# Running two stages' products, then two stages' outputs, in a fused attention and mixture kernel on one Trainium2 core

## The chip, the core and the metric

One NeuronCore of a Trainium2 chip runs the whole program. Its engines work side by side, each through its own list of instructions in the order in which the program wrote them: PE (matrix products, with weight loads shown as PEld), DVE (element-wise work, reads the products' accumulators), ACT (activations, copies and rounding, reads the accumulators too), POOL (element-wise work on SBUF) and SP (which issues most DMAs). An engine whose next instruction waits for a semaphore holds up everything behind it in its own list. The metric is device time of one execution in microseconds (us).

## The reference: what is computed

Three layers follow each other: block-causal attention, a mixture of eight experts with weights from a Sinkhorn-like normalisation, and a squared-ReLU feed-forward layer.

```python
# attention: batch 4, heads 8, 576 positions, head size 64, blocks of 64
attn = softmax over allowed blocks of (q k^T / 8);  x = (attn v) as [2304, 512]
# mixture ("layer one"): 8 experts, each 512 -> 1024 -> 512
P = exp(x @ w_gate - max); 8 rounds of normalising rows and columns of P
out = sum over e of P[:, e:e+1] * (relu(x @ w1[e]) @ w2[e])
# feed-forward ("layer two"): 512 -> 2048 -> 512, weights given as float64
g = relu(x @ w_in) ** 2
return g @ w_out
```

## The kernel before

**Tiling.** The 2304 tokens are cut into three groups of 768 (`NG = 3`), each of six tiles of 128 tokens (`GT = 6`). A *stage* takes one group and one slice of 256 hidden columns: 32 stages per group in layer one (8 experts times 4 slices), 8 in layer two. The list `stages` has 120 entries S: 0 to 95 are layer one (three groups of 32), 96 to 119 layer two (three groups of 8).

**A stage** has two halves on PE. First come seven *products* (function `product`), one for each of the seven terms of a Strassen-like scheme (`PRODUCTS`, called m1, m2, m6, m7, m4, m5, m3 in the order in which they run). Each is six matmuls of 384 columns, L346 to L348 twice, since both operands are split into a rounded part and a remainder (`ah`, `al` for the weights, `x` for the input). Then come six *output tiles* (function `output`), each of six matmuls of 512 columns, L401 to L403 twice, that multiply the hidden tile `h` by the second weight `b`.

**What the products feed.** Each product lies in one PSUM bank until its reader is through. m1 is copied to SBUF by ACT (L357); the others are read by DVE additions (L352), which form sums u2, u3, u4 and four tiles `c`. Each `c` becomes hidden values (`hidden`): in layer one ACT applies ReLU with rounding (L314) and DVE forms the remainder (L315). In layer two three of the four `c` of a stage take two more steps on ACT, ReLU and square (L320, L321), before the rounding (L324); the first one is squared by DVE (L323). DVE's remainder there is L325. Remainders are put in the queue `wait` and written into DVE's list a little later: `product` empties the queue after m1, m2, m6, m7, m4 and m5, and `output` takes one entry at tile `PUTOFF = 3`.

**Where products lie.** `Turns` hands out banks to products in rotation over five places: four single banks (`sc00` to `sc11`) and, as fifth, the pool `ps`, whose four banks are shared with the output tiles, themselves in rotation. A product therefore needs, four times out of five, that the product five before it has been read; an output tile needs that the holder of the bank four before it in the shared pool has been read.

**What else runs.** Weights come as float32 and are split on chip. `conv_a` splits one of the seven first-weight combinations for a stage: ACT rounds (L197) and POOL forms the remainder (L198). `sums` forms four combinations on POOL (L181). `conv_b` splits half of the second weight (ACT L205, POOL L206); `load` brings the raw weights, one buffer for `w2` and two for `w1`. `form` builds the next group's seven input combinations (POOL L265, ACT L271, L272 on POOL or DVE). `conv64` turns layer two's float64 weights into float32 during layer one (DVE L222 to L240, POOL L225).

**What sets the order.** The program keeps a list `pieces`; each piece is a product or an output tile with the helpers attached to it. `fill` walks through it, and after each piece takes steps of the queues `gate`, `slow` (`conv64`, every `SLOW`-th piece), `forming` (`fetch` and `form`, every `pace`-th piece) and `side` (`stage_work`: `conv_b`, `sums`, loading). From stage 5 on the order is `RUNS`: the seven products of stage S, then the six output tiles of stage S-1. In `products(S)`, the weights of stage S+1 are split one product behind the product that used the same buffer (`conv_a(S + 1, ...)`).

Of the kernel before, what the change touches and what calls it, by code (L numbers as in the profile page):

```python
# [25 lines left out]
NG = 3  # L26
GT = NTILE // NG
GN = 64 * GT
NMOE = 32
NST = 40  # L30
# [13 lines left out]
PRODUCTS = [(1, 0, 0), (2, 1, 1), (6, 4, 4), (7, 5, 5), (4, 2, 6), (5, 3, 3), (3, 6, 2)]  # L44
# [54 lines left out]
PUTOFF = 3  # L99
# [3 lines left out]
DLO = (0, 3, 6, 9, 12)  # L103

GATE = 1

SLOW = 4

# [16 lines left out]
def fused_kernel(ctx: ExitStack, tc: tile.TileContext, q, k, v, wg, w1, w2, u1, u2, ident, out):  # L125
# [24 lines left out]
    stages = [  # L150
        (g, s, layer * NG + g)
        for layer, (s0, s1) in enumerate(((0, NMOE), (NMOE, NST))) for g in range(NG) for s in range(s0, s1)
    ]
# [17 lines left out]
    def sums(S):  # L171
        if S >= len(stages):
            return
        r = raw["w1", S].rearrange("p (f d) -> p f d", f=2)
        a11, a12, a21, a22 = r[:, 0, 0:256], r[:, 0, 256:512], r[:, 1, 0:256], r[:, 1, 256:512]
        t = wsum[S] = rawp.tile([128, 4, 256], F32, tag="sum", name="sum")
        for z, (o, x, y, op) in enumerate((
            (0, a21, a22, ALU.add), (1, t[:, 0], a11, ALU.subtract), (2, a11, a21, ALU.subtract),
            (3, a12, t[:, 1], ALU.subtract),
        )):  # L180
            nc.gpsimd.tensor_tensor(out=t[:, o], in0=x, in1=y, op=op)  # L181
            if z == 1:
                yield
        yield
# [146 lines left out]
    def in_runs(S):  # L331
        return EARLY < S < NG * NST

    def product(S, j):
        g, s, q = stages[S]
        m, ia, ib = PRODUCTS[j]
        if j == 0:
            ht[S] = [[hpool.tile([128, 2 * GN], F32R, tag=f"h{f}{z}", name=f"h{f}{z}", bufs=2) for z in range(2)]
                     for f in range(2)]
            while q not in formed:  # L340
                assert step_of(forming)
        p = extra["ps"].tile([128, 512], F32, tag="g", name="m")[:, :GN]
        ah, al = wa[S, ia]
        bh, bl = (t[:, ib] for t in xop[q % 2])
        for k2 in range(2):
            nc.tensor.matmul(p, ah[:, k2], bh[:, k2], start=(k2 == 0), stop=False)  # L346
            nc.tensor.matmul(p, ah[:, k2], bl[:, k2], start=False, stop=False)  # L347
            nc.tensor.matmul(p, al[:, k2], bh[:, k2], start=False, stop=(k2 == 1))  # L348

        def add(tag, other, pool=tmp):  # L350
            t = pool.tile([128, GN], F32, tag=tag, name=tag)
            nc.vector.tensor_tensor(out=t, in0=p, in1=cur[other], op=ALU.add)  # L352
            return t

        if m == 1:
            cur["m1"] = tmp.tile([128, GN], F32, tag="mu", name="m1")
            nc.scalar.activation(out=cur["m1"], in_=p, func=ACTF.Copy)  # L357
            flush_wait()
        elif m == 2:
            x = add("c", "m1", cpool)  # L360
            flush_wait()
            hidden(S, 0, 0, x)
        elif m == 6:
            cur["u2"] = add("u2", "m1")
            flush_wait()
        elif m == 7:
            cur["u3"] = add("u3", "u2")
            flush_wait()
        elif m == 4:
            x = add("c", "u3", cpool)  # L370
            flush_wait()
            hidden(S, 1, 0, x)
        elif m == 5:
            cur["u4"] = add("mu", "u2")
            x = add("c", "u3", cpool)
            flush_wait()
            hidden(S, 1, 1, x)
        else:
            x = add("c", "u4", cpool)
            if not in_runs(S):  # L380
                flush_wait()
            hidden(S, 0, 1, x)
# [31 lines left out]
    def output(S, t):  # L414
        g, s, q = stages[S]
        if not in_runs(S + 1):
            flush_wait()
        elif wait and (t == PUTOFF or S == NG * NST - 2 and t == 1):
            wait.popleft()()
        while S not in ready_b:  # L420
            assert step_of(side)
        first = q == 0 and s < 8
        if q == 0 and s == 8:
            drain(gate)
        a = acc[1 if first and s >= 4 else q % 2][:, t]
        if S == len(stages) - 1 and t == GT - 1:
            last_tile(S, t, a, (g * GT + t) * 128)
            return
        p = ps.tile([128, 512], F32, tag="g", name="y")
        terms(p, S, t, slice(0, 512))  # L430

        e = s // 4
        tile_no = g * GT + t
        pe = prob[:, tile_no, e % NEXP:e % NEXP + 1]
        if s == NMOE:
            nc.vector.tensor_copy(out=a, in_=p)
        elif first and s % 4 == 0:
            nc.scalar.activation(out=a, in_=p, func=ACTF.Copy)
        elif s == 0:
            nc.scalar.activation(out=a, in_=p, func=ACTF.Copy, scale=pe)  # L440
        elif s > NMOE or first:
            nc.vector.tensor_tensor(out=a, in0=p, in1=a, op=ALU.add)
        else:
            if q == 0 and s == 8:
                nc.scalar.activation(out=a, in_=a, func=ACTF.Copy, scale=prob[:, tile_no, 0:1])
            nc.vector.scalar_tensor_tensor(out=a, in0=p, scalar=pe, in1=a, op0=ALU.mult, op1=ALU.add)  # L446
            if q == 0 and s == 8 + t // 2:
                nc.vector.scalar_tensor_tensor(
                    out=a, in0=acc[1][:, t], scalar=prob[:, tile_no, 1:2], in1=a, op0=ALU.mult, op1=ALU.add
                )  # L450
        if s == NMOE - 1:
            late.append((q, t))
        if len(late) > (2 if s == NMOE - 1 else 0):
            x2(*late.popleft())
        if s == NST - 1:
            r0 = tile_no * 128
            nc.sync.dma_start(out=out[r0:r0 + 128, :], in_=a)
# [4 lines left out]
    def piece(fn, us=0.0, need=None):  # L462
        pieces.append((need, us, fn))

    def products(S):
        res = []
        for j in range(7):
            def fn(j=j):
                product(S, j)
                if j == 0:  # L470
                    load("w1", S + 2)
                else:
                    conv_a(S + 1, PRODUCTS[j - 1][1])
                if j == 6:
                    conv_a(S + 1, PRODUCTS[6][1])
            res.append((0, 1.03, fn))
        return res

    def outputs(S):
        return [(0, 1.37, lambda t=t: output(S, t)) for t in range(GT)]  # L480

    def task(gen):
        piece(lambda: side.append(gen))
# [6 lines left out]
    def step_of(queue):  # L490
        while queue:
            if next(queue[0], "end") != "end":
                return True
            queue.popleft()
        return False
# [8 lines left out]
    def stage_work(S):  # L504

        conv_b(S, 0)
        if S + 1 < len(stages):
            yield from sums(S + 1)
            summed.add(S + 1)
        conv_b(S, 1)  # L510
        load("w2", S + 1)
        ready_b.add(S)
        yield

    pace = [1]

    def begin(S):
        side.append(stage_work(S))
        g, s, q = stages[S]
        layer = s >= NMOE  # L520
        at, every = FORM[layer]
        if s - (NMOE if layer else 0) == at and q + 1 < 2 * NG:
            forming.append(fetch(q + 1))
            pace[0] = every

    for S in range(len(stages) + 1):
        a = products(S) if S < len(stages) else []
        b = outputs(S - 1) if S else []
        if a:
            piece(lambda S=S: begin(S))  # L530
        for z in WEAVE if S <= EARLY else RUNS if in_runs(S) else BLOCKS:
            src = a if z == "m" else b
            if src:
                pieces.append(src.pop(0))
        pieces += a + b
        if S == EARLY:
            split = len(pieces)
    pos = [0]
    beat = [0]

    def fill(us, end):
        while us > 0 and pos[0] < end:
            need, cost, fn = pieces[pos[0]]
            if need is not None and need not in formed:
                return us
            fn()
            pos[0] += 1
            us -= cost
            if cost:
                beat[0] += 1  # L550
                for _ in range(GATE):
                    step_of(gate)
                if beat[0] % SLOW == 0 and not gate:
                    step_of(slow)
                if beat[0] % pace[0] == 0:
                    step_of(forming)
                step_of(side)
        return us

# [473 lines left out]
```

## Time and profile before

| | before |
|---|---|
| median of 3 runs | 2058.68 us (2058.38 to 2059.91) |
| the profiled execution's own time | 2058.25 us |
| its span, first to last instruction | 2056.5 us |
| TensorE's granted clock over the span | 1.000 (2.4 GHz) |
| PE busy | 2040.9 us, 99% of the span |
| DVE, POOL, ACT busy | 1620.9 us (79%), 1586.1 us (77%), 988.5 us (48%) |
| share of PE in the chain that ended last | 95% |

The span covers attention with the first stages woven into it, up to about 310 us, and then a regular stretch of products and output tiles up to the end. Busy time of PE counts overlapping matmuls once; one matmul's duration (335 or 391 ns) is longer than the distance from its start to the next one's start, so distances between starts tell more than durations. "Idle before" is time in which the engine did nothing, with what ended it.

### The profile page before, as it was taken

Reading aid. Unit: us, or ns where it says so; the run is one execution under the profiler, and the core shown is the slowest. Engines: PE = TensorE matmul, PEld = TensorE weight load, DVE = VectorE, ACT = ScalarE, POOL = GpSimd, SP = SyncE. Lnnn points to the kernel's source line nnn. Section 1 sums busy time; section 2 is a strip of 40 time slices with the busy share of each in tenths; the row PEclk is TensorE's granted clock in tenths of the full one; section 3 lists DMA queues with packets and bytes.
Section 4 is the critical chain, followed back from the end, with each engine's and each line's share of the span. In section 5 each row is a group of like instructions: output and inputs, shape, how many; then the busy total and the mean of one; then the engine's idle time right before and its main releaser. Section 6 shows DMA issues by size and latency. Waiting matters only on the chain.

```text
span 2056.5 us, 34155 instructions
## 1 busy us (share of the span) xinstructions
PE 2040.9 (99%) x11614; PEld 1813.2 (88%) x11614; DVE 1620.9 (79%) x2864; ACT 988.5 (48%) x2439; POOL 1586.1 (77%) x1786
## 2 busy tenths in 40 slices
PE   8999999999999999999999999999999999999999
PEld 5677898998999899899899999989989998998998
DVE  7887788888887678788888777888887677777776
ACT  8977444344343434334434343433443446656554
POOL 4564577798888778778888777878887778979874
PEclk9999999999999999999999999999999999999999
DMA  6543212322222322232223233233222123232311
GB/s 186 149 131 93 64 62 92 124 78 96 95 77 100 116 82 93 92 114 93 86 79 103 77 118 103 78 115 106 78 77 88 62 83 111 75 123 67 108 62 51
DMA packets 80862, 194.70 MB, mean 95 GB/s; under 512 B 26160, under 2 KB 27568, under 8 KB 80688
## 3 DMA queue, kind: packets, MB, share of 16 engines
q1 hardware_dynamic: 80544, 192.39, 28.3%
q8 instruction: 91, 1.49, 0.3%
q14 instruction: 83, 0.68, 0.1%
q10 hardware_dynamic: 144, 0.13, 0.0%
HBM read 169.95 MB, written 20.97 MB: 93 GB/s over the span
## 4 chain that ended last, share of the span: by engine, by line
PE 95%; DVE 3%; ACT 1%; issue 1%; POOL 0%; DMA 0%; SPq 0%; ACTq 0%; POOLq 0%; DVEq 0%
PE y L401 16%; PE y L402 16%; PE y L403 16%; PE m L346 14%; PE m L348 14%; PE m L347 14%; PE pv L750 1%; PE sc L626 1%; PE T L706 1%; DVE mx L645 1%; DVE pb L683 1%; ACT pb L667 0%; DVE nm L656 0%; PE x2t L392 0%; DVE sm L688 0%
## 5 line engine op out<-in xcount | busy, mean ns | idle before, releaser
L346 PE MATMUL m<-x,ah 128*128 128x384 f32 x1680 | 566.0, 337 | 0.4 <-DVE c L352 0.3
L401 PE MATMUL y<-b,h 128*128 128x512 f32 x1442 | 564.6, 392 | 0.9 <-DVE c L352 0.9
L403 PE MATMUL y<-b,h 128*128 128x512 f32 x1442 | 563.8, 391 | 0.0
L348 PE MATMUL m<-x,al 128*128 128x384 f32 x1680 | 563.5, 335 | 0.0
L402 PE MATMUL y<-b,h 128*128 128x512 f32 x1442 | 563.3, 391 | 0.0
L347 PE MATMUL m<-x,ah 128*128 128x384 f32 x1680 | 562.7, 335 | 0.0
L206 POOL TENSOR_TENSOR b<-raww,b 128x512 fp32r<-128x512 f32 x240 | 326.6, 1361 | 299.9 <-ACT b L205 296.6
L446 DVE SCALAR_TENSOR_TENSOR acc<-y,prob,acc 128x512 f32<-128x512 f32 x516 | 380.4, 746 | 132.1 <-PE y L403 127.4
L198 POOL TENSOR_TENSOR al<-sum,ah 128x256 fp32r<-128x256 f32 x480 | 392.4, 837 | 33.2 <-ACT ah L197 13.6
L357 ACT ACTIVATE m<-m 128x384 f32<-128x384 f32 x120 | 59.1, 492 | 634.1 <-PE m L348 634.1
L346 PEld LDWEIGHTS m<-x,ah 128*128 128x128 f32 x1680 | 315.7, 188 | 8.1 <-issue 0.5
L198 POOL TENSOR_TENSOR al<-raww,ah 128x256 fp32r<-128x256 f32 x360 | 307.0, 853 | 17.8 <-ACT ah L197 11.4
L403 PEld LDWEIGHTS y<-b,h 128*128 128x128 f32 x1442 | 270.7, 188 | 56.7
L347 PEld LDWEIGHTS m<-x,ah 128*128 128x128 f32 x1680 | 315.5, 188 | 4.7
L401 PEld LDWEIGHTS y<-b,h 128*128 128x128 f32 x1442 | 271.1, 188 | 54.4 <-DVE c L352 1.0
L402 PEld LDWEIGHTS y<-b,h 128*128 128x128 f32 x1442 | 270.9, 188 | 52.5
L348 PEld LDWEIGHTS m<-x,al 128*128 128x128 f32 x1680 | 315.4, 188 | 0.0
L315 DVE SCALAR_TENSOR_TENSOR h<-c,h 128x384 fp32r<-128x384 f32 x384 | 303.6, 791 | 3.7 <-ACT h L314 3.3
L314 ACT ACTIVATE h<-c 128x384 fp32r<-128x384 f32 x384 | 201.3, 524 | 179.0 <-DVE c L352 169.8
L197 ACT ACTIVATE ah<-sum 128x256 fp32r<-128x256 f32 x480 | 185.1, 409 | 128.0 <-POOL sum L181 119.0
L181 POOL TENSOR_TENSOR sum<-raww 128x256 f32<-128x256 f32 x240 | 198.7, 828 | 0.0
L352 DVE TENSOR_TENSOR c<-m,m 128x384 f32<-128x384 f32 x120 | 66.8, 557 | 106.2 <-ACT b L205 95.2
(117 smaller groups left out, 2416.3 us busy)
## 6 DMA issues: line engine op xcount, KB each, us to landing
raww<-w_t SPq DMA_DIRECT2D x192, 512.0 KB, 3.5
raww<-w1f SPq DMA_DIRECT2D x24, 512.0 KB, 3.5
raww<-w2f SPq DMA_DIRECT2D x24, 512.0 KB, 3.3
q<-q_d SPq DMA_DIRECT2D x15, 576.0 KB, 4.0
raw<-w_in_bits SPq DMA_DIRECT2D x16, 512.0 KB, 5.0
raw<-w_out_bits SPq DMA_DIRECT2D x16, 512.0 KB, 4.6
acc<-xd SPq DMA_DIRECT2D x30, 256.0 KB, 4.7
v<-v_p SPq DMA_DIRECT2D x16, 320.0 KB, 3.8
```

The costliest lines, as they stand in the source:

```text
L181: nc.gpsimd.tensor_tensor(out=t[:, o], in0=x, in1=y, op=op)
L198: nc.gpsimd.tensor_tensor(out=lo, in0=src, in1=hi.bitcast(F32), op=ALU.subtract)
L206: nc.gpsimd.tensor_tensor(out=lo[:, f], in0=src, in1=hi[:, f].bitcast(F32), op=ALU.subtract)
L314: nc.scalar.activation(out=hh, in_=x3, func=ACTF.Relu)
L315: wait.append(lambda: nc.vector.scalar_tensor_tensor(out=hl, in0=x3, scalar=0.0, in1=hh.bitcast(F32), op0=ALU.max, op1=ALU.subtract,))
L346: nc.tensor.matmul(p, ah[:, k2], bh[:, k2], start=(k2 == 0), stop=False)
L347: nc.tensor.matmul(p, ah[:, k2], bl[:, k2], start=False, stop=False)
L348: nc.tensor.matmul(p, al[:, k2], bh[:, k2], start=False, stop=(k2 == 1))
L401: nc.tensor.matmul(p, hh, bh[:, f, cols], start=(f == 0), stop=False)
L402: nc.tensor.matmul(p, hh, bl[:, f, cols], start=False, stop=False)
L403: nc.tensor.matmul(p, hl, bh[:, f, cols], start=False, stop=(f == 1))
L446: nc.vector.scalar_tensor_tensor(out=a, in0=p, scalar=pe, in1=a, op0=ALU.mult, op1=ALU.add)
```

## The change

From stage 12 on, stages go in pairs (S, S+1), S even: seven products of S, seven of S+1, then six output tiles of S and six of S+1. The numbers of instructions on PE, DVE and POOL stay as they are; their order changes. The `conv_a` of the odd stage stays in the products of the even one, that of the next even stage moves to the output tiles of the even one, and the products of the odd stage carry none. `sums` of the next pair's odd stage goes between the two runs of output tiles. Within pairs the steps of `slow` and `forming` are taken beside output tiles alone (`kind` "t"): `slow` at every second one, `forming` at every fifth in layer one and every second in layer two (`TFORM`). Two remainders are written at tiles 1 and 3 of the first run of output tiles of a pair (and of stage 10).

```diff
+TFORM = {False: 5, True: 2}
+
+TWO = 12
...
+    def is_pair(S):
+        return TWO <= S < NG * NST and S % 2 == 0
+
+    def twice(S):
+        return is_pair(S) or S in (TWO - 2, NG * NST - 2)
...
-        elif wait and (t == PUTOFF or S == NG * NST - 2 and t == 1):
+        elif wait and (t in (1, PUTOFF) if twice(S) else t == PUTOFF):
             wait.popleft()()
...
                 if j == 0:
                     load("w1", S + 2)
-                else:
+                elif not is_pair(S - 1):
                     conv_a(S + 1, PRODUCTS[j - 1][1])
-                if j == 6:
+                if j == 6 and not is_pair(S - 1):
                     conv_a(S + 1, PRODUCTS[6][1])
...
         conv_b(S, 0)
-        if S + 1 < len(stages):
-            yield from sums(S + 1)
-            summed.add(S + 1)
+        if S + 1 not in summed:
+            yield from add_up(S + 1)
+        else:
+            yield
+            yield
         conv_b(S, 1)
...
             pace[0] = every
+            tpace[0] = TFORM[layer]
...
+    def both(S):
+
+        for z in (S, S + 1):
+            piece(lambda z=z: begin(z))
+            pieces.append((None, 0.0, lambda: kind.__setitem__(0, "m")))
+            pieces.extend(products(z))
+        pieces.append((None, 0.0, lambda: kind.__setitem__(0, "t")))
+        ys = outputs(S)
+        for t, (need, us, fn) in enumerate(ys):
+            def more(t=t, fn=fn):
+                fn()
+                for j in (t, t + 1) if t == GT - 1 else (t,):
+                    conv_a(S + 2, PRODUCTS[j][1])
+            pieces.append((need, us, more))
+        task(add_up(S + 3))
+        pieces.extend(outputs(S + 1))
+        pieces.append((None, 0.0, lambda: kind.__setitem__(0, "")))
...
+        if is_pair(S):
+            if due is not None:
+                pieces += outputs(due)
+                due = None
+            both(S)
+            S += 2
+            continue
...
-                if beat[0] % SLOW == 0 and not gate:
-                    step_of(slow)
-                if beat[0] % pace[0] == 0:
-                    step_of(forming)
+                if kind[0] == "t":
+                    turns[0] += 1
+                    if turns[0] % 2 == 0 and not gate:
+                        step_of(slow)
+                    if turns[0] % tpace[0] == 0:
+                        step_of(forming)
+                elif kind[0] == "":
...
```

The lines of the changed program are shifted: PE's products are L356 to L358 there, its output tiles L411 to L413, ACT's copy of m1 L367, DVE's additions L362.

PE's list where the last stage's products begin, before: `y_24171` is an output tile of the stage two before it, `m_24183` the last stage's m1.

```order
L403 MATMUL y_24171<-b0_23847,h01_23832 128x512
L401 MATMUL y_24171<-b0_23847,h10_23833 128x512
L402 MATMUL y_24171<-b1_23848,h10_23833 128x512
L403 MATMUL y_24171<-b0_23847,h11_23834 128x512
L346 MATMUL m_24183<-x01_3738,ah_24038 128x384
L347 MATMUL m_24183<-x11_3739,ah_24038 128x384
```

The same place of the changed program: `m_24158` is the seventh product of the stage just before, `m_24182` the last stage's m1.

```order
L358 MATMUL m_24158<-x01_3738,al_24004 128x384
L356 MATMUL m_24158<-x01_3738,ah_24003 128x384
L357 MATMUL m_24158<-x11_3739,ah_24003 128x384
L358 MATMUL m_24158<-x01_3738,al_24004 128x384
L356 MATMUL m_24182<-x01_3738,ah_24088 128x384
L357 MATMUL m_24182<-x11_3739,ah_24088 128x384
```

The six output tiles that stood ahead of m1 are gone from there; the odd stage's products follow the even stage's with nothing between them.

DVE's list at the same place, before: from the `c` of the seventh product (`c_24117`) to the last stage's first two additions; `acc1` rows empty output tiles, `h` rows are remainders.

```order
L352 TENSOR_TENSOR c_24117<-m_24110,mu_24098 128x384
L442 TENSOR_TENSOR acc1_3737<-y_24130,acc1_3737 128x512
L442 TENSOR_TENSOR acc1_3737<-y_24138,acc1_3737 128x512
L442 TENSOR_TENSOR acc1_3737<-y_24146,acc1_3737 128x512
L325 TENSOR_TENSOR h11_24009<-c_24100,h10_24008 128x6x64
L442 TENSOR_TENSOR acc1_3737<-y_24155,acc1_3737 128x512
L442 TENSOR_TENSOR acc1_3737<-y_24163,acc1_3737 128x512
L442 TENSOR_TENSOR acc1_3737<-y_24171,acc1_3737 128x512
L325 TENSOR_TENSOR h01_24007<-c_24117,h00_24006 128x6x64
L352 TENSOR_TENSOR c_24206<-m_24199,m1_24190 128x384
L323 SCALAR_TENSOR_TENSOR c_24206<-c_24206 128x384
L352 TENSOR_TENSOR u2_24217<-m_24210,m1_24190 128x384
```

And in the changed program, from the `c` of the seventh product (`c_24165`) on.

```order
L362 TENSOR_TENSOR c_24165<-m_24158,mu_24146 128x384
L329 TENSOR_TENSOR h11_24063<-c_24148,h10_24062 128x6x64
L329 TENSOR_TENSOR h01_24061<-c_24165,h00_24060 128x6x64
L362 TENSOR_TENSOR c_24206<-m_24199,m1_24189 128x384
L327 SCALAR_TENSOR_TENSOR c_24206<-c_24206 128x384
L362 TENSOR_TENSOR u2_24217<-m_24210,m1_24189 128x384
```

The six rows that emptied output tiles have moved away; the two remainders stay and stand directly ahead of the odd stage's first addition.

ACT's list at that place of the changed program, from the even stage's last hidden tile on.

```order
L324 ACTIVATE c_24165<-c_24165 128x384
L325 ACTIVATE c_24165<-c_24165 128x384
L328 ACTIVATE h00_24060<-c_24165 128x6x64
L201 ACTIVATE ah_24170<-sum_24015 128x256
L201 ACTIVATE ah_24174<-sum_24015 128x256
L367 ACTIVATE m1_24189<-m_24182 128x384
```

ACT's rows stand here as they did before (L320 to L324, twice L197, L357); what has moved is PE's m1 that the last row reads.

## Rows read from the trace of the kernel before

**Rows 1.** The page: engines' busy time, and the chain that ended last.

```profile
PE 2040.9 (99%) x11614; PEld 1813.2 (88%) x11614; DVE 1620.9 (79%) x2864; ACT 988.5 (48%) x2439; POOL 1586.1 (77%) x1786
...
PE 95%; DVE 3%; ACT 1%; issue 1%; POOL 0%; DMA 0%; SPq 0%; ACTq 0%; POOLq 0%; DVEq 0%
```

**Rows 2.** The page's costliest groups: busy us, mean ns, idle before and its end.

```profile
L346 PE MATMUL m<-x,ah 128*128 128x384 f32 x1680 | 566.0, 337 | 0.4 <-DVE c L352 0.3
L401 PE MATMUL y<-b,h 128*128 128x512 f32 x1442 | 564.6, 392 | 0.9 <-DVE c L352 0.9
...
L446 DVE SCALAR_TENSOR_TENSOR acc<-y,prob,acc 128x512 f32<-128x512 f32 x516 | 380.4, 746 | 132.1 <-PE y L403 127.4
```

**Rows 3.** PE's instructions in order: start us, duration us, instruction.

```profile
1719.14 0.33 PE L346 MATMUL m<-x,ah 128*128 128x384 f32 x1
...
1982.75 0.33 PE L346 MATMUL m<-x,ah 128*128 128x384 f32 x1
...
1983.82 0.33 PE L346 MATMUL m<-x,ah 128*128 128x384 f32 x1
...
1990.06 0.39 PE L401 MATMUL y<-b,h 128*128 128x512 f32 x1
...
2029.27 0.33 PE L346 MATMUL m<-x,ah 128*128 128x384 f32 x1
...
2038.65 0.39 PE L401 MATMUL y<-b,h 128*128 128x512 f32 x1
...
2051.58 0.28 PE L401 MATMUL y<-b,h 128*128 128x256 f32 x1
```

**Rows 4.** ACT in order in the layer-two stage that begins at 1982.75 us.

```profile
1984.01 0.49 ACT L357 ACTIVATE m<-m 128x384 f32<-128x384 f32 x1 [4.41 <-PE m L348]
...
1989.18 0.53 ACT L320 ACTIVATE c<-c 128x384 f32<-128x384 f32 x1 [0.17 <-DVE c L352]
...
1992.88 0.51 ACT L320 ACTIVATE c<-c 128x384 f32<-128x384 f32 x1
...
1993.98 0.52 ACT L324 ACTIVATE h<-c 128x384 fp32r<-128x384 f32 x1
1994.41 0.71 ACT L197 ACTIVATE ah<-sum 128x256 fp32r<-128x256 f32 x2
```

**Rows 5.** DVE in order in the same stage and after it.

```profile
1985.11 0.56 DVE L352 TENSOR_TENSOR c<-m,m 128x384 f32<-128x384 f32 x1 [1.00 <-ACT b L205]
1985.70 1.10 DVE L323 SCALAR_TENSOR_TENSOR c<-c 128x384 f32<-128x384 f32 x1
...
1987.40 0.56 DVE L325 TENSOR_TENSOR h<-c,h 128x384 fp32r<-128x384 f32 x1
...
1990.86 0.90 DVE L325 TENSOR_TENSOR h<-c,h 128x384 fp32r<-128x384 f32 x1 [0.63 <-ACT h L324]
1991.87 0.56 DVE L352 TENSOR_TENSOR c<-m,mu 128x384 f32<-128x384 f32 x1
1992.34 0.68 DVE L442 TENSOR_TENSOR acc<-y,acc 128x512 f32<-128x512 f32 x1
...
1994.98 1.15 DVE L325 TENSOR_TENSOR h<-c,h 128x384 fp32r<-128x384 f32 x1
```

**Rows 6.** PE, DVE and ACT in the layer-one stage that begins at 1344.18 us.

```profile
1344.18 0.33 PE L346 MATMUL m<-x,ah 128*128 128x384 f32 x1
...
1346.54 0.56 DVE L352 TENSOR_TENSOR c<-m,m 128x384 f32<-128x384 f32 x1 [0.94 <-ACT b L205]
...
1348.93 1.22 DVE L240 SCALAR_TENSOR_TENSOR hc<-sq,a 128x512 f32<-128x512 f32 x1
...
1353.37 0.56 DVE L352 TENSOR_TENSOR c<-m,mu 128x384 f32<-128x384 f32 x1
...
1354.39 0.71 ACT L197 ACTIVATE ah<-sum 128x256 fp32r<-128x256 f32 x2
```

**Rows 7.** Groups by line and shape, POOL: busy us, mean ns, idle before.

```profile
L198 POOL TENSOR_TENSOR al<-sum,ah 128x256 fp32r<-128x256 f32 x480 | 392.4, 837 | 33.2 <-ACT ah L197 13.6 <-DVE turned L782 5.7 <-PE gm L927 5.0
L206 POOL TENSOR_TENSOR b<-raww,b 128x512 fp32r<-128x512 f32 x240 | 326.6, 1361 | 299.9 <-ACT b L205 296.6 <-DMA acc<-xd 3.2
L181 POOL TENSOR_TENSOR sum<-raww 128x256 f32<-128x256 f32 x240 | 198.7, 828 | 0.0
L272 POOL TENSOR_TENSOR x<-f,x 128x384 fp32r<-128x384 f32 x25 | 28.6, 1149 | 0.0
```

More of the change, by code (lines that the diff above doesn't have):

```diff
@@ L515, in fused_kernel @@
     pace = [1]
+    kind = [""]
+    tpace = [1]
     def begin(S):
@@ L524, in begin, with add_up @@
             pace[0] = every
-    for S in range(len(stages) + 1):
+            tpace[0] = TFORM[layer]
[15 more added lines that the diff above has]
+        pieces.append((None, 0.0, lambda: kind.__setitem__(0, "")))
+    def add_up(S):
+        if S < len(stages):
+            yield from sums(S)
+            summed.add(S)
+    due = None
+    S = 0
+    while S <= len(stages):
+        if is_pair(S):
+            if due is not None:
+                pieces += outputs(due)
+                due = None
+            both(S)
+            S += 2
+            continue
         a = products(S) if S < len(stages) else []
-        b = outputs(S - 1) if S else []
+        b = outputs(due) if due is not None else []
         if a:
@@ L531, in fused_kernel @@
         for z in WEAVE if S <= EARLY else RUNS if in_runs(S) else BLOCKS:
-            src = a if z == "m" else b
-            if src:
-                pieces.append(src.pop(0))
+            p = a if z == "m" else b
+            if p:
+                pieces.append(p.pop(0))
         pieces += a + b
@@ L537, in fused_kernel @@
             split = len(pieces)
+        due = S
+        S += 1
     pos = [0]
     beat = [0]
+    turns = [0]
     def fill(us, end):
@@ L552, in fill @@
                     step_of(gate)
-                if beat[0] % SLOW == 0 and not gate:
-                    step_of(slow)
-                if beat[0] % pace[0] == 0:
-                    step_of(forming)
+                if kind[0] == "t":
[5 more added lines that the diff above has]
+                elif kind[0] == "":
+                    if beat[0] % SLOW == 0 and not gate:
+                        step_of(slow)
+                    if beat[0] % pace[0] == 0:
+                        step_of(forming)
                 step_of(side)
```

## The prediction

> **What bounds the kernel now.** I read the page first: PE is busy for 99% of the span, and the chain that ended last is 95% PE [rows 1]. The reader should see that no other engine comes near. Then the costliest groups: the idle time ahead of PE's first matmul of a product is 0.4 us over 1680 instructions, ahead of an output tile's first 0.9 us over 1442 [rows 2]. So PE waits for nobody, and an edit can gain only by making PE's own matmuls follow each other faster; it can lose by any new wait. Third, PE in order of time, by distances between starts. In the stage that begins at 1982.75 us the first six matmuls take 1.07 us to the seventh (1983.82), the other 36 take 6.24 us up to the first output tile (1990.06), 0.1733 us each [rows 3]. Late in the last run of output tiles 57 matmuls take 12.93 us (2038.65 to 2051.58), 0.2268 us each [rows 3]. At these two paces a stage would be 42 x 0.1733 + 36 x 0.2268 = 15.44 us. Twenty stages take 310.13 us (1719.14 to 2029.27) [rows 3], 15.506 us each. Each stage thus pays 0.066 us for its two changes of kind, product to output tile and back; half of it stands in the rows, since six matmuls at 0.1733 would be 1.04 us and not 1.07. Last come ACT and DVE in one stage of either layer [rows 4 to 6], to see how far they run behind PE, since the change takes away the output tiles during which they catch up.
>
> **Part one: half of the changes of kind go.** Stages 12 to 119 are 54 pairs, and each pair saves one change each way: 54 x 0.066 = 3.6 us. With the rounding of the two paces it is between 2.5 and 4.5. I take 3.6. The page "TensorE: Matmul & The Clock Gate" of the Trainium skill, section "Back-to-back issue gap", gives the warm gap as N/2.4 + 2.5 ns, a function of the columns alone; by that nothing is saved by joining runs. The trace has both paces some 11 ns above that formula and the first matmuls of a run above their own pace, so I go by the rows and keep the formula's answer as a rival.
>
> **Part two: layer one, 42 pairs.** All times from here on are counted from the start of a pair and are estimates from the rows. Seven products take 7.31 us (1982.75 to 1990.06), each further one 1.04. The odd stage's sixth product starts at 7.31 + 5 x 1.04 = 12.51; four times in five it needs the bank of the odd stage's m1, which ACT has to copy first. The run of output tiles starts at 14.59, and its fifth tile, at 1.37 us a tile (15.506 - 7.31 = 8.20 for six), at 20.07; it needs the first tile's bank, which DVE has to empty. In the layer-one stage that begins at 1344.18 ACT is through with its work for the products at 1355.10, 10.92 us after the start [rows 6]. The odd m1 stands right behind that in ACT's list; at 0.49 us [rows 4] it is copied by 11.4, 1.1 us early. DVE needs from its first c to the end of its last 7.39 us (1346.54 to 1353.93), a conversion of 1.22 us among them [rows 6]. 11.4 + 7.4 = 18.8, and emptying the first tile, 0.75 us [rows 2], ends at 19.55, 0.5 us early. The change takes the conversions away from the products, so there is more room than that. Weights: the odd stage's are split by POOL in the even stage's products, where 7 x 0.84 + 2 x 1.36 = 8.6 us of work [rows 7] meet 7.3 us of PE, but each is used seven products after its buffer came free. I cost layer one at nothing. If the cover fails by 0.1 us a pair it costs 4.2 us.
>
> **Part three: layer two, 12 pairs.** Here ACT has three triples per stage (ReLU, square, round). In the stage that begins at 1982.75 the first triple starts at 1989.18, the last ends at 1994.50, and two roundings of weights end at 1995.12 [rows 4], 12.37 us after the start, though PE had left the products at 7.31. Before, ACT caught up under the output tiles; its next m1 waited 4.41 us for PE [rows 4]. In the changed order the odd m1 is ready at about 8.6 but stands behind the triples: it is copied at 12.37 + 0.49 = 12.86. The sixth product, due at 12.51, waits 0.35 us in four pairs of five. Then DVE: its first c needs m1's copy. From first c to the end of the last it took 1985.11 to 1992.43 = 7.32 us [rows 5], a chain in which squaring (1.10), hidden rounding on ACT and the remainder (0.90, after a triple) follow each other. So the odd stage's last c ends at 12.86 + 7.32 = 20.18, the first output tile is emptied at 20.18 + 0.68 = 20.86 [rows 5], and the fifth, due at 20.07, starts 0.79 us late. The earlier 0.35 us is contained in this. Afterwards DVE empties a tile in 0.68 us against 1.37 us of PE and catches up, remainders included: the odd stage's last one, after a triple that ends near 21.9 and two more tiles, is done near 23.6 and needed near 24. Cost: 12 x 0.79 = 9.5 us. In one pair of five the odd stage's last product lies in the pool shared with the output tiles, and then the fourth tile, due at 18.70, waits for 20.18: 1.48 instead of 0.79, in 12 / 5 = 2.4 pairs, 1.7 us more. Bounds per pair: if that remainder takes 0.56 us, as the one at 1987.40 does, and the copy overlaps its predecessor by 0.1, 0.35 us are left, 4 us in all; if it and the next one take 1.15 us, as the one at 1994.98 does [rows 5], the tiles behind are late too, some 1.3 us a pair, 16 us in all.
>
> **Part four: forming in layer two.** In two of three groups, three of four pairs carry the next input's forming beside output tiles. The second of these three has the most, seven operations in POOL's list of the changed program. POOL there starts on the next weights when ACT is free, at about 21.9, and has 7 x 0.84 + 4 x 0.83 + 7 x 1.15 = 17.2 us to do [rows 7], up to 39.1; the pair ends at 31.8. The next pair's POOL begins 7.3 us late, finishes one b and one al at 7.3 + 1.36 + 0.84 = 9.5, and the odd stage's first product needs that al with its third matmul at 7.66; the third product waits again behind the second b. Some 2.1 us late instead of 0.8, in two pairs: 2.6 us. The bounds are 0 (POOL's gaps before absorb it) and 12 us (all four heavier pairs lose 3 us).
>
> **Sum.** 2058.25 (the profiled execution) - 3.6 + 9.5 + 1.7 + 2.6 = 2068.45. The median of the runs is 0.43 us above the profiled execution: 2068.9 us. The first twelve stages, attention and the last tiles with their DMAs keep their order, and I cost them at nothing.
>
> **The rivals.** First, the backlog of layer two is hidden: ACT's triples end earlier, or products find another free bank, and only part one remains. 2058.68 - 3.6 = 2055.1 us. For it speaks that in the stage before the last product, begun by PE at about 1989.0, is read only at 1991.87 and PE does not wait [rows 3, 5]; against it that the rows of ACT reach 5 us past the products and ACT's list is unchanged there. It decides from the point at which m1's copy comes before 12.0 and the first tile is emptied before 20.1. Second, POOL becomes the bound in the six forming pairs: the upper bound of part four, 2068.9 - 2.6 + 12 = 2078 us. For it: al, b, sums and forming make 31.8 us per such pair (14 x 0.84 + 4 x 1.36 + 8 x 0.83 + 7 x 1.15) against 31.0 of PE; against: only the pair with seven operations reaches that. Third, joining runs saves nothing, since the slow first matmuls belong to something that each stage's beginning brings with it: 2068.9 + 3.6 = 2072.5 us. This is where the formula of "TensorE: Matmul & The Clock Gate" would lead, and the rows speak against it: the last two stages' output tiles already follow each other without a break and run at one pace from the tenth matmul on. Fourth, waits of layer two half as long as I work out, so that 3 to 4 us of them meet 3.6 us of saving: no change, about 2059.
>
> **How the numbers follow.** The forecast, waits in layer two of 8 to 18 us: 0.66, with 2063 to 2074 as its own range. Rival one 0.14, rival two 0.07, rival three 0.05, rival four 0.08. What a measurement of this kernel can tell from no change is 0.2%, 4.1 us. Slower by more: the forecast, rivals two and three, less the low edge of the forecast, 0.75. Within it: rival four and most of rival one, whose 3.6 us lie just inside, 0.17. Faster: the rest, 0.08. The range takes in rival one at its lower end and the forecast's upper edge with rival three: 2055 to 2076.
>
> **What would show it.** In the changed trace, right: layer one's pairs take 2 x 15.506 - 0.066 = 30.95 us with PE never idle; layer two's take 31.7 or more, with PE held ahead of the odd stage's sixth product by ACT's m1 and ahead of the fifth (or fourth) output tile by DVE's emptying or its last c; ACT's odd m1 starts about 12.4 us into such a pair; in the third forming pair of a group PE waits for al. Wrong: layer-two pairs of 30.95 us; then part three fails, and the step to look at is the copy of m1. If part one is wrong, the odd stage's products begin with slow matmuls as well. If part two is wrong, PE waits in layer one.

## The result, and the profile after

The changed kernel takes 2078.17 us, median of 5 runs (2077.61 to 2078.74), against 2058.68 us (2058.32 to 2059.91) of the kernel before: a ratio of 1.0094, 95% interval 1.0083 to 1.0105. It is slower by 19.5 us. Forecast were 2068.9 us, with 2055 to 2076 as the range: the direction was right and the size 9.3 us short. The profiled execution's span is 2076.0 us at a granted clock of 1.000.

The page of the changed kernel: busy time, the chain that ended last, and PE's groups (busy us, mean ns, idle before and its end).

```profile
PE 2045.1 (99%) x11614; PEld 1809.7 (87%) x11614; DVE 1634.8 (79%) x2864; ACT 976.1 (47%) x2439; POOL 1596.0 (77%) x1786
...
PE 86%; DVE 6%; ACT 4%; issue 2%; POOL 1%; DMA 0%; SPq 0%; DVEq 0%; ACTq 0%; POOLq 0%
...
L411 PE MATMUL y<-b,h 128*128 128x512 f32 x1442 | 565.5, 392 | 9.2 <-DVE acc L452 4.5
L358 PE MATMUL m<-x,al 128*128 128x384 f32 x1680 | 563.4, 335 | 5.7 <-POOL al L202 5.7
L356 PE MATMUL m<-x,ah 128*128 128x384 f32 x1680 | 565.8, 337 | 1.5 <-ACT m L367 0.7
```

PE is still "99% busy", so its busy share doesn't show that something is wrong. The chain does: PE's share fell from 95% to 86% [rows 1]. So does PE's idle time ahead of these three lines: it is 16.4 us, where the first matmul of a product and that of a tile had 1.3 together before [rows 2]. Who ended most of it is named: DVE's emptying, POOL's `al`, ACT's m1; of the 4.7 us ahead of tiles that the first line leaves unnamed, 3.9 ended with a `c` of DVE.

**Layer one** keeps its promise. PE in order (start, duration) through one pair of the changed kernel:

```profile
1305.06 0.33 PE L356 MATMUL m<-x,ah 128*128 128x384 f32 x1
...
1319.64 0.39 PE L411 MATMUL y<-b,h 128*128 128x512 f32 x1
...
1336.01 0.33 PE L356 MATMUL m<-x,ah 128*128 128x384 f32 x1
```

A pair takes 30.95 us, which is 2 x 15.506 less 0.066 [rows 3], and no matmul in it waits. (Five pairs are 1.0 or 1.8 us longer, since transposes stand between their tiles; stages of the kernel before are longer by the same at those places.) Only the first pair of all, at stage 12, waits: the third product of stage 13 needs an `al` that POOL came to late, behind the four sums that it forms within this pair.

```profile
380.64 0.44 PE L358 MATMUL m<-x,al 128*128 128x384 f32 x1 [0.94 <-POOL al L202]
```

**Layer two.** An ordinary pair, from 2008.64 us on: PE first.

```profile
2008.64 0.33 PE L356 MATMUL m<-x,ah 128*128 128x384 f32 x1
...
2020.62 0.33 PE L356 MATMUL m<-x,ah 128*128 128x384 f32 x1
2021.37 0.44 PE L356 MATMUL m<-x,ah 128*128 128x384 f32 x1
...
2028.36 0.39 PE L411 MATMUL y<-b,h 128*128 128x512 f32 x1
2030.01 0.50 PE L411 MATMUL y<-b,h 128*128 128x512 f32 x1 [0.81 <-DVE acc L452]
2030.81 0.40 PE L411 MATMUL y<-b,h 128*128 128x512 f32 x1
2031.50 0.40 PE L411 MATMUL y<-b,h 128*128 128x512 f32 x1
...
2041.04 0.33 PE L356 MATMUL m<-x,ah 128*128 128x384 f32 x1
```

The pair takes 32.40 us, 1.45 more than 30.95. Half-products follow each other at 0.52 us, but the odd stage's sixth product (2021.37) comes 0.75 after the matmul before it in this list: 0.23 late. Half-tiles follow at 0.68, but the fifth tile (2030.01) comes 1.65 after: 0.97 late. Behind each wait some 0.11 more is lost (0.80 instead of 0.69 at 2030.81); 0.23 + 0.97 + 2 x 0.11 = 1.42 of the 1.45. Now ACT in the same pair, then DVE, then POOL:

```profile
2019.80 0.53 ACT L328 ACTIVATE h<-c 128x384 fp32r<-128x384 f32 x1
2020.23 0.71 ACT L201 ACTIVATE ah<-sum 128x256 fp32r<-128x256 f32 x2
2020.85 0.47 ACT L367 ACTIVATE m<-m 128x384 f32<-128x384 f32 x1
```

```profile
2021.35 0.56 DVE L362 TENSOR_TENSOR c<-m,m 128x384 f32<-128x384 f32 x1 [0.43 <-ACT m L367]
...
2027.10 1.59 DVE L329 TENSOR_TENSOR h<-c,h 128x384 fp32r<-128x384 f32 x1 [0.84 <-ACT h L328]
2028.80 0.56 DVE L362 TENSOR_TENSOR c<-m,mu 128x384 f32<-128x384 f32 x1
2029.27 0.68 DVE L452 TENSOR_TENSOR acc<-y,acc 128x512 f32<-128x512 f32 x1
```

```profile
2026.29 0.74 POOL L185 TENSOR_TENSOR sum<-raww,sum 128x256 f32<-128x256 f32 x1
2026.98 1.30 POOL L210 TENSOR_TENSOR b<-raww,b 128x512 fp32r<-128x512 f32 x1
```

m1 of the odd stage is copied 12.21 us into the pair, behind the even stage's last triple and two roundings, where [rows 4] had given 12.37. DVE's chain then runs as in [rows 5] but for one row: the remainder took 1.59 us, not 0.90, while POOL converted half of the second weight beside it. The last pair has no such conversion beside its remainder, which there took:

```profile
2059.50 0.56 DVE L329 TENSOR_TENSOR h<-c,h 128x384 fp32r<-128x384 f32 x1 [0.84 <-ACT h L328]
```

and its fifth tile doesn't wait.

**Forming pairs.** Four pairs, not two, wait for POOL's `al`: those that begin at 1775.4, 1809.3, 1908.5 and 1942.5, by 2.4, 1.1, 2.4 and 1.05 us. In all they take 2.9, 2.9, 3.0 and 2.1 us more than 30.95, since tiles wait for DVE in each of them too. POOL in the first of them, and the two matmuls of PE that wait:

```profile
1778.48 1.35 POOL L269 TENSOR_TENSOR f<-acc 128x384 f32<-128x384 f32 x1
...
1781.09 1.01 POOL L276 TENSOR_TENSOR x<-acc,x 128x384 fp32r<-128x384 f32 x1
1782.06 1.29 POOL L210 TENSOR_TENSOR b<-raww,b 128x512 fp32r<-128x512 f32 x1
1783.31 1.74 POOL L202 TENSOR_TENSOR al<-raww,ah 128x256 fp32r<-128x256 f32 x2
```

```profile
1784.41 0.45 PE L358 MATMUL m<-x,al 128*128 128x384 f32 x1 [1.19 <-POOL al L202]
...
1787.38 0.45 PE L358 MATMUL m<-x,al 128*128 128x384 f32 x1 [0.61 <-POOL al L202]
```

POOL begins on the weights 6.7 us into the pair, and the odd stage's first and third products wait. The pair behind it finds POOL late again, by 5.4 us (`b` at 1814.64), and waits once for `al` and, for longer, at a tile:

```profile
1814.64 1.61 POOL L210 TENSOR_TENSOR b<-raww,b 128x512 fp32r<-128x512 f32 x1
```

```profile
1819.94 0.44 PE L358 MATMUL m<-x,al 128*128 128x384 f32 x1 [0.57 <-POOL al L202]
...
1830.72 0.50 PE L411 MATMUL y<-b,h 128*128 128x512 f32 x1 [1.48 <-DVE c L362]
```

### The profile page after: what moved, and what is told of

Same layout as the page of the kernel before. It is cut to its first block, busy times and chain, and to the rows that moved or that the text cites. A ratio compares the mean times of both kernels' runs of the same rounds, so it can differ in the third digit from the quotient of the medians.

```text
span 2076.0 us, 34533 instructions
## 1 busy us (share of the span) xinstructions
PE 2045.1 (99%) x11614; PEld 1809.7 (87%) x11614; DVE 1634.8 (79%) x2864; ACT 976.1 (47%) x2439; POOL 1596.0 (77%) x1786
## 4 chain that ended last, share of the span: by engine, by line
PE 86%; DVE 6%; ACT 4%; issue 2%; POOL 1%; DMA 0%; SPq 0%; DVEq 0%; ACTq 0%; POOLq 0%
PE y L411 15%; PE y L413 15%; PE y L412 15%; PE m L356 12%; PE m L358 12%; PE m L357 12%; PE pv L807 1%; PE sc L683 1%; PE T L763 1%; DVE c L362 1%; ACT h L328 1%; ACT c L325 1%; DVE h L329 1%; ACT c L324 1%; DVE mx L702 1%
## 5 line engine op out<-in xcount | busy, mean ns | idle before, releaser
L411 PE MATMUL y<-b,h 128*128 128x512 f32 x1442 | 565.5, 392 | 9.2 <-DVE acc L452 4.5
L358 PE MATMUL m<-x,al 128*128 128x384 f32 x1680 | 563.4, 335 | 5.7 <-POOL al L202 5.7
L356 PE MATMUL m<-x,ah 128*128 128x384 f32 x1680 | 565.8, 337 | 1.5 <-ACT m L367 0.7
L413 PE MATMUL y<-b,h 128*128 128x512 f32 x1442 | 562.4, 390 | 0.0
L357 PE MATMUL m<-x,ah 128*128 128x384 f32 x1680 | 562.0, 335 | 0.0
L210 POOL TENSOR_TENSOR b<-raww,b 128x512 fp32r<-128x512 f32 x240 | 317.0, 1321 | 176.4 <-ACT b L209 176.1
L202 POOL TENSOR_TENSOR al<-sum,ah 128x256 fp32r<-128x256 f32 x480 | 403.7, 861 | 58.3 <-ACT ah L201 35.2
L319 DVE SCALAR_TENSOR_TENSOR h<-c,h 128x384 fp32r<-128x384 f32 x384 | 334.5, 880 | 11.3 <-ACT h L318 5.9
L367 ACT ACTIVATE m<-m 128x384 f32<-128x384 f32 x120 | 57.9, 483 | 603.1 <-PE m L358 603.1
L411 PEld LDWEIGHTS y<-b,h 128*128 128x128 f32 x1442 | 270.8, 188 | 68.3 <-DVE acc L452 7.6
L356 PEld LDWEIGHTS m<-x,ah 128*128 128x128 f32 x1680 | 315.4, 188 | 9.6 <-ACT m L367 3.6
L358 PEld LDWEIGHTS m<-x,al 128*128 128x128 f32 x1680 | 315.3, 188 | 8.5 <-POOL al L202 8.4
L413 PEld LDWEIGHTS y<-b,h 128*128 128x128 f32 x1442 | 270.7, 188 | 56.9
L357 PEld LDWEIGHTS m<-x,ah 128*128 128x128 f32 x1680 | 315.5, 188 | 2.6
L201 ACT ACTIVATE ah<-sum 128x256 fp32r<-128x256 f32 x480 | 177.6, 403 | 9.3 <-POOL sum L185 9.3
L209 ACT ACTIVATE b<-raww 128x512 fp32r<-128x512 f32 x240 | 149.2, 622 | 15.7 <-DMA raww<-w_t 8.9
```

Source lines behind the costliest of these rows:

```text
L202: nc.gpsimd.tensor_tensor(out=lo, in0=src, in1=hi.bitcast(F32), op=ALU.subtract)
L210: nc.gpsimd.tensor_tensor(out=lo[:, f], in0=src, in1=hi[:, f].bitcast(F32), op=ALU.subtract)
L319: wait.append(lambda: nc.vector.scalar_tensor_tensor(out=hl, in0=x3, scalar=0.0, in1=hh.bitcast(F32), op0=ALU.max, op1=ALU.subtract,))
L411: nc.tensor.matmul(p, hh, bh[:, f, cols], start=(f == 0), stop=False)
L413: nc.tensor.matmul(p, hl, bh[:, f, cols], start=False, stop=(f == 1))
```

## The experiments

Two causes were at hand for layer two: the chain from ACT's late m1 through DVE (with POOL's `b` lengthening it), and POOL's forming. Rivals were a slow layer one, and something of the pairing itself. Of each kernel the edit against the changed one is shown, or what is new in it where it keeps earlier edits; all times are medians, ratios against the kernel before.

**POOL's conversion moved off DVE's remainder.** In odd stages of layer two the second `conv_b` comes ahead of the four sums (ACT's half of it and the loading of the next second weight move along).

```diff
+        if S >= NG * NMOE and S % 2:
+            yield
+            conv_b(S, 1)
+            load("w2", S + 1)
+            ready_b.add(S)
+            yield
+            yield from add_up(S + 1)
+            return
         if S + 1 not in summed:
```

> Theory P (POOL holds DVE up): the remainder of the odd stage's m4 takes 1.59 us in the changed kernel because POOL's second b of the odd stage (1.30 us) runs just then; with that b ahead of the four sums, the remainder falls to about 1.0 us or less, the first output tiles are emptied about 0.5 us sooner, and ten layer-two pairs lose 0.5 us less each: about 2073 us. Rival (the chain is ACT's alone, the remainder's length is hidden): 2078 us.

2071.41 us (2071.02 to 2071.82), ratio 1.0061, 1.0047 to 1.0075: 6.8 us of the 19.5 are gone, by an exchange in POOL's list; ACT's m1 still comes 12.21 us into ordinary pairs. DVE and POOL in an ordinary pair of it:

```profile
2021.08 0.90 DVE L329 TENSOR_TENSOR h<-c,h 128x384 fp32r<-128x384 f32 x1 [0.84 <-ACT h L328]
```

```profile
2020.82 0.74 POOL L185 TENSOR_TENSOR sum<-raww 128x256 f32<-128x256 f32 x1
2021.53 1.05 POOL L185 TENSOR_TENSOR sum<-raww,sum 128x256 f32<-128x256 f32 x1
```

Beside a sum the remainder takes 0.90, and such a pair takes 31.70 us: it loses 0.75, where 0.79 had been predicted with that 0.90. The waits for `al` stayed as they were (2.4, 0.9, 2.4 and 0.85 us).

**Squares left out.** Of layer two's even stages the Square of three of the four hidden tiles is left out, so ACT has 1.7 us less ahead of the odd m1; such a kernel computes something else and serves for its time alone.

```diff
-                nc.scalar.activation(out=x, in_=x, func=ACTF.Square)
+                if S % 2:
+                    nc.scalar.activation(out=x, in_=x, func=ACTF.Square)
```

> Leaves out the square of three of four hidden tiles in the even stages of layer two (its output is not the reference's). Theory A (ACT's triples ahead of the odd m1 set the waits): ACT is through 1.6 us sooner, the wait ahead of the odd stage's sixth product goes and those ahead of the fourth or fifth output tile shrink to 0.2 us or less; the waits for al, about 6.6 us in four pairs, stay: about 2064 us. Rival (DVE has 14.5 us of work in 14.6 us of products and falls behind by itself): only the 0.33 us waits go, 2074 us or more.

2067.42 us (2066.32 to 2068.74), ratio 1.0042, 1.0028 to 1.0055. An ordinary pair of it, PE, then ACT's odd m1:

```profile
2001.20 0.33 PE L357 MATMUL m<-x,ah 128*128 128x384 f32 x1
...
2032.21 0.33 PE L357 MATMUL m<-x,ah 128*128 128x384 f32 x1
```

```profile
2011.74 0.47 ACT L368 ACTIVATE m<-m 128x384 f32<-128x384 f32 x1
```

m1 is copied 10.54 us into the pair, and ordinary pairs take 31.01 us without a wait, though the remainder still takes 1.58: it comes early enough. The total missed its 2064: the four waits for `al` grew to 2.7 and 1.4 us, and pairs with forming lost time at tiles too. In the pair from 1772.6 POOL begins on the weights 6.7 us in, as before, but the `al` that the third product needs takes 1.04 us instead of 0.72, with a remainder of DVE now beside it.

**Forming left out.** Layer two's second and third group inputs are neither fetched nor formed; this kernel too serves for its time alone.

```diff
-            forming.append(fetch(q + 1))
+            if layer:
+                formed.add(q + 1)
+            else:
+                forming.append(fetch(q + 1))
```

> Leaves out fetching and forming the inputs of layer two's second and third group (its output is not the reference's). Theory F (forming makes POOL late in four pairs): no wait for al in layer two; those pairs then lose what ordinary pairs lose, 1.45 us, or 2.2 us in one of five: about 2073 us. Rival (POOL is late by its conversions alone): al waits of 2.4 us stay in the same pairs and the time stays above 2077 us.

2072.93 us (2072.55 to 2073.17), ratio 1.0068, 1.0054 to 1.0082. All waits for `al` in layer two are gone and its pairs are ordinary ones (32.4 us, or 33.1 with the last product in the shared pool). Forming thus costs 5.2 us on top of what the pairs lose anyway.

**Pairs in layer one alone**, with stage 13's sums made one stage ahead.

```diff
-        return TWO <= S < NG * NST and S % 2 == 0
+        return TWO <= S < NG * NMOE and S % 2 == 0
...
-        pieces.extend(outputs(S + 1))
+        if S + 2 < NG * NMOE:
+            pieces.extend(outputs(S + 1))
...
+        if S == TWO:
+            task(add_up(TWO + 1))
...
+            if S == NG * NMOE:
+                due = S - 1
```

> Pairs in layer one alone (stages 12 to 95), with the sums of stage 13 made one stage ahead. Theory (layer one hides everything and each pair saves 0.066 us): 42 pairs save 2.8 us, no wait of PE from stage 12 on: 2055.9 us. Rival (joining runs saves nothing): 2058.7 us. If layer one had hidden losses too: above 2059 us.

2055.66 us, median of 11 runs (2055.52 to 2055.95), ratio 0.9985, 0.9976 to 0.9994: 3.05 us faster than the kernel before, and the only complete kernel here that is faster. 42 x 0.066 is 2.8. The page of this kernel shows that PE waits no more than before:

```profile
PE 95%; DVE 3%; ACT 1%; issue 1%; POOL 0%; DMA 0%; SPq 0%; ACTq 0%; POOLq 0%; DVEq 0%
...
L356 PE MATMUL m<-x,ah 128*128 128x384 f32 x1680 | 564.9, 336 | 0.4 <-DVE c L362 0.3
L411 PE MATMUL y<-b,h 128*128 128x512 f32 x1442 | 564.1, 391 | 0.9 <-DVE c L362 0.9
L358 PE MATMUL m<-x,al 128*128 128x384 f32 x1680 | 562.3, 335 | 0.0
```

**Forming's remainders on DVE**, all but the last one of each input (the trace has 26 on DVE and 2 on POOL), with pairs in both layers, the sums of stage 13 ahead, and `b` first as above.

```diff
-                rest.pop()(nc.vector if z - 1 in DLO else nc.gpsimd)
+                rest.pop()(nc.vector if q > NG or z - 1 in DLO else nc.gpsimd)
```

> The pairs of the changed kernel in both layers, with three edits: the four sums for stage 13 are made one stage ahead; in layer two's odd stages POOL's second conversion of w2 comes ahead of the four sums; and all forming remainders of layer two run on VectorE, none on POOL. Theory (POOL is late in four pairs by the work of the two group inputs, VectorE's ordinary loss is 0.75 us a pair): the waits of TensorE for POOL's second operands go or fall under 0.5 us, ordinary pairs take 31.7 us and the ones with the last product in the shared pool about 32.4; 2055.7 from the run with pairs in layer one alone, less 12 x 0.066, plus 12 x 0.75, plus about 1.5: 2065 us, between 2063 and 2067. Rival (POOL is late by its conversions, whoever forms): the four waits for POOL's operands stay at 1 to 2.4 us each, about 2070 us.

2065.41 us (2065.28 to 2066.22), ratio 1.0034, 1.0021 to 1.0046, as expected. One wait for `al` of 0.43 us is left; seven pairs take 31.6 to 31.7 us. That is still 9.8 us above pairs in layer one alone.

**Weights ahead.** On top of that kernel, five of the seven first-weight conversions of layer two's odd stages are made beside the tiles of the pair before.

```diff
+EXTRA = {4: ("second", "a4"), 5: ("cv", "hc"), 2: ("cv", "sq"), 3: ("cv", "a"), 6: ("cv", "raw8")}
+    def early(S, i):
+        return S > NG * NMOE and S % 2 and i in EXTRA
...
+        if early(S, i):
+            pool, tag = EXTRA[i]
+            t = extra[pool].tile([128, 2, 2, 128], F32R, tag=tag, name="ahl")
+            hi, lo = t[:, 0], t[:, 1]
...
+                for j in {2: (2,), 3: (3,), 4: (4,), 5: (5, 6)}.get(t, ()):
+                    if early(S + 3, PRODUCTS[j][1]):
+                        conv_a(S + 3, PRODUCTS[j][1])
```

> The kernel of e7_dve_forms, in which five of the seven conversions of first weights by ScalarE in layer two's odd stages are made beside the tiles of the pair before, into buffers of their own. Theory (the ordinary pair loses its time because ScalarE copies m1 of the odd stage late, and VectorE's chain follows it): the copy of m1 starts some 1.8 us earlier, near 10.5 us into the pair; no wait is left ahead of the sixth product nor the fifth tile in ordinary pairs, which take 31.0 us; about 2055 us (2053.5 to 2058), as fast as pairs in layer one alone or up to 0.8 us faster. Rival (VectorE itself has too much to do in layer two, whenever m1 comes): the fifth tile still waits 0.3 us or more in ordinary pairs, 2060 us or more.

2068.55 us (2066.99 to 2070.08), ratio 1.0045, 1.0031 to 1.0059: a miss by 13.5 us. The mechanism of ordinary pairs held: m1 at 10.98, pairs of 31.2 to 31.3 us. But six pairs now wait for `al` by 0.7 to 1.6 us, and tiles of the same six wait for DVE by another 0.6 to 1.1; in all these pairs lose 1.8 to 2.9 us. POOL in one of them, and PE:

```profile
1773.84 1.74 POOL L212 TENSOR_TENSOR ahl<-sum,ahl 128x256 fp32r<-128x256 f32 x2
1775.54 1.01 POOL L279 TENSOR_TENSOR f<-acc 128x384 f32<-128x384 f32 x1
...
1779.24 1.02 POOL L279 TENSOR_TENSOR f<-f,acc 128x384 f32<-128x384 f32 x1
1780.21 1.28 POOL L220 TENSOR_TENSOR b<-raww,b 128x512 fp32r<-128x512 f32 x1
1781.44 1.75 POOL L212 TENSOR_TENSOR al<-raww,ah 128x256 fp32r<-128x256 f32 x2
```

```profile
1782.23 0.45 PE L368 MATMUL m<-x,al 128*128 128x384 f32 x1 [1.39 <-POOL al L212]
```

A conversion has a half on POOL as well: the five (`ahl`) and the forming (`f`) stand ahead of the first `al` that PE needs.

**Weights ahead, no forming.** The same edit as above (`formed.add`) on the kernel with the weights ahead, for its time alone.

> The kernel of e8_weights_ahead, which leaves out the fetching and forming of the second and third group's inputs of layer two; its output isn't the reference's. The run with the weights ahead lost 1.3 to 2.9 us in six pairs and 0.25 us in the others. Theory (its six slow pairs are those in which POOL and VectorE form inputs, and moving the conversions forward only brought their waits forward): all pairs take 31.2 to 31.3 us, the waits for POOL's operands are gone; 2055.66 - 12 x 0.066 + 12 x 0.3: about 2058.5 us, between 2057 and 2060. Rival (the moved conversions and their buffers themselves make POOL late): waits for POOL's operands of 0.7 us or more stay in some pairs, 2063 us or more.

2056.45 us (2055.45 to 2057.23), ratio 0.9988, 0.9978 to 0.9997: all waits for `al` are gone, so the six slow pairs were due to the forming. It came out 2 us under the forecast, since half of the pairs have no wait at all (30.95 us), most others lose 0.2, and one with its last product in the shared pool 1.07.

**Neither backlog.** Pairs in both layers with the three edits of the kernel with forming's remainders on DVE, without the Squares and without the forming, for its time alone.

> The kernel of e7_dve_forms without the work that each of the two theories blames: it leaves out the Square of three of four hidden tiles in layer two's even stages (ScalarE's backlog), and the fetching and forming of the second and third group's inputs of layer two (POOL's backlog); its output isn't the reference's. Theory (these two backlogs are the whole loss of layer two): no wait over 0.1 us in any of layer two's pairs, which take 31.0 us; 2055.66 from pairs in layer one alone, less 12 x 0.066, plus 12 x 0.06: about 2055.5 us, between 2054.5 and 2057. Rival (a third thing is lost in layer two's pairs that the two have covered, POOL's order or the switch of layers): 2059 us or more.

2055.00 us, median of 10 runs (2054.79 to 2056.56), ratio 0.9981, 0.9972 to 0.9991. Pairs of layer two take 30.95 us, two of them 31.1 and the first 31.97; in the first, two groups of four transposes (`x2t`) stand between the tiles, as they do at the switch of layers in the kernel before too, and nothing waits. The page, where the idle time is what it was before [rows 2]:

```profile
L412 PE MATMUL y<-b,h 128*128 128x512 f32 x1442 | 564.3, 391 | 0.9 <-DVE c L363 0.9
L357 PE MATMUL m<-x,ah 128*128 128x384 f32 x1680 | 564.8, 336 | 0.4 <-DVE c L363 0.3
...
L359 PE MATMUL m<-x,al 128*128 128x384 f32 x1680 | 562.2, 335 | 0.0
```

Nothing of the loss remains: ACT's backlog with DVE's chain behind it, the forming, and at stage 12 the late sums are all of it.

## Why the prediction was wrong

**Part one, right.** The excess at a change of kind is what it was, and it comes once per pair: 0.066 us saved in each, 30.95 us per pair. The rival that joining runs saves nothing falls with the 3.05 us of pairs in layer one alone.

**Part two, right but for its first pair.** 41 pairs wait for nothing. At stage 12 the pairing begins without the sums that every later pair finds ready: 0.94 us of idle time, 1.2 to 1.3 us over PE's pace, which I had not counted. That the sums are the cause is shown by their being made a stage earlier: the wait is gone.

**Part three, the step that failed.** The chain "From first c to the end of the last" of 7.32 us carried over a remainder of 0.90 us from [rows 5] as if it belonged to the operation. It took 1.59, since the new order puts POOL's conversion of `b` beside it, and the chain took 8.01. The 0.69 more is about the difference between 0.79 and 1.45 per pair (0.66), and the exchange in POOL's list gave 0.70 back per pair, 6.8 us in all. That the two agree so closely is in part luck: m1 came 0.16 us early (12.21 for 12.37), and the 0.11 lost behind the tile's wait, which I had not counted, made up for most of that. The rest came out: the wait ahead of the sixth product 0.23 for 0.35, the fourth tile in the shared pool 0.72 dearer for 0.69. Only ten of the twelve pairs lose the full amount; the first loses 0.5 and the last 0.4 us. The whole term is 16.9 us, from the run without forming (2072.93 less 2055.66, less 1.2 for stage 12, plus the 12 x 0.066 that the pairs of layer two save), where 11.2 were predicted. My upper bound held a remainder of 1.15, the longest in [rows 5], and was 16 us.

**Part four, mechanism right, count wrong.** POOL begins 6.7 us into the third forming pair, for 7.3 predicted, and PE waits there 2.4 us for 2.1. But POOL doesn't recover within that pair, because it forms again beside its tiles: the pair behind waits another 1.1. The two such runs of pairs cost 5.2 us for 2.6. How large the term is depends on the other one: with ordinary pairs free of waits (Squares left out), the forming pairs and their neighbours lose some 11.4 us (2067.42 less 2055.66, less 1.2, plus 0.8), at tiles as well as for `al`. A pair that has waited for POOL doesn't wait again for ACT's m1, though its tiles still wait for DVE (0.4 to 1.75 us); and the two terms, 16.9 and 11.4 alone, cost 22.1 together (16.9 + 5.2), not their sum.

**The sum.** Missed were 5.7 in part three, 2.6 in part four and 1.2 at stage 12: 9.5, against the 9.3 us between 2068.9 and 2078.17. Rival two had the right time, 2078, by luck: POOL is not the bound in six pairs, and the forming makes a quarter of the loss (5.2 of 22). (Its sum of POOL's work per pair is 31.9, not 31.8.)

## What to carry to other kernels

A duration read from a trace belongs to the order in which it was measured. Where a change moves a DVE operation with both inputs in SBUF, look in the new order at what POOL does beside it, and price it by the row with that neighbour. And do half of such a change: here pairs pay where ACT has slack (layer one), and cost far more than they save in layer two, where ACT and DVE had used the removed gap to catch up.

## What the hardware showed that I had not expected

**DVE and POOL take turns, and the remainder ends 0.41 us after the POOL operation it meets.** All 56 remainders of the changed kernel's layer two that start while POOL is at work end 0.41 to 0.43 us after POOL's operation. In the changed kernel `b` ended at 2028.28 and the remainder at 2028.69; in the kernel with `b` first the sum ended at 2021.56 and the remainder at 2021.98, and the next sum took 1.05 us instead of 0.74. POOL and DVE of the kernel before show the same beside an `al`, with the remainder of [rows 5] that ends at 1991.76:

```profile
1990.62 0.73 POOL L198 TENSOR_TENSOR al<-raww,ah 128x256 fp32r<-128x256 f32 x1
1991.31 1.61 POOL L206 TENSOR_TENSOR b<-raww,b 128x512 fp32r<-128x512 f32 x1
```

The 40 that start while POOL is idle take 0.55 to 0.56. Of the 840 additions that read PSUM (L362) none takes more than 0.56, whatever POOL does. The page "SBUF — State Buffer" of the Trainium skill, section "SBUF: two separate sides", states that a DVE operation with two SBUF inputs and a POOL operation that reads SBUF lock a port pair in turn, each for its whole length. These traces agree: the remainder is through only behind the POOL operation, and its delay (1.03 and 0.34 us in the two kernels) is what was left of that (1.18 and 0.48) less some 0.15.

**A wait costs more than its length.** The matmul right behind one that waited is some 0.10 to 0.11 us late too; 0.2 of the 1.45 us of an ordinary pair stand behind its two waits. PE's weight loads behind the wait at 2030.01:

```profile
2030.01 0.19 PEld L411 LDWEIGHTS y<-b,h 128*128 128x128 f32 x1 [1.23 <-DVE acc L452]
2030.12 0.19 PEld L412 LDWEIGHTS y<-b,h 128*128 128x128 f32 x1
```

The load of the matmul that waits starts with that matmul and not 0.23 us ahead of it, as the load at 2031.27 does for the matmul at 2031.50; the matmul takes 0.50 instead of 0.39 us, and the next load comes 0.11 us behind its start. No run tried to move the load ahead of the wait.
